# Offset weight tiles, two conversions moved beside the last block, and the second output step's sums moved into the h stage

## The chip, the cores and the metric

The kernel runs on one core of one Trainium2 chip. The metric is the device time of one execution in microseconds (us), lower is better. Five engines work side by side, each through its own list of instructions in order: PE (matmuls, with PEld for the weight loads), DVE and POOL (elementwise), ACT (elementwise, activations, casts) and SP, which here only issues transfers (DMAs). An instruction waits until what it reads has been written and what it overwrites has been read.

## The reference

The reference chains three pieces: an attention over a window of 64 keys (4 batches, 8 heads, 576 positions, head size 64), a bilinear layer and a SiLU layer, all on 2304 tokens of width 512.

```
scores = q @ k^T / 8, masked to 0 <= i - j < 64
x  = softmax(scores) @ v                    # 2304 x 512
x2 = ((x @ w1) * (x @ w2)) @ w3 @ w_out     # 512 -> 1024 -> 1024 -> 512
h  = x2 @ w_in                              # 512 -> 2048
y  = (h * sigmoid(h)) @ w_out2              # 2048 -> 512
```

`q`, `k`, `v` are single precision. The weights arrive in double precision and are turned into single precision on the chip.

## The kernel before

**Precision.** A single-precision product is made of rounded halves: each operand is split into a high part and a low remainder, and a product takes three passes (high by high, low by high, high by low). A weight tile therefore holds both halves of a 128x512 piece, and a matmul has 128 rows, 128 columns of weights and 384 tokens (256 output columns in the last stage).

**Conversion of a double-precision weight.** A tile of 64-bit words comes from DRAM (`l0`, `l1` issue the load, L145). ACT takes two ACTIVATEs over it (L220 writes `cv_b`, L225 writes `cv_r`), DVE masks and merges the bits (L228, then SCALAR_TENSOR_TENSOR at L884), POOL adds the remainder (L887). For `w_out2` the function `convert(n, at, places)` does this for a pair of tiles, adds the sums that the seven-product scheme wants (`cv_t`, `cv_u`) and stores all seven pieces to the DRAM scratch `t32`. Its pieces are entered in the table `jobs` at times from `at - 2` (first load) to `at + 7` (last store).

**Stages.** (1) to about 95 us: `w3` and `w_out` are folded into one weight `wp`, attention begins. (2) Six blocks of 384 tokens (`phase_a`): sixteen chains `ab` (x by w1 and w2, L693), whose even members are copied out by ACT (L707) and whose odd ones DVE multiplies with that copy; `p` is the split product; then four chains `x2` (L723) with `wp`, stored to DRAM. The chains rotate through four PSUM banks, so a chain waits until the copy or product of the fourth chain before it has read its bank. Attention of the next block is woven in; the last block (5) has none, and there `hooks5` brings in the first operands of the next stage: at unit 0 it loads `x2` of the earlier blocks (`xra`, `xe`) and the first `w_in` tile (`r`). A block has 24 units: one per `ab` chain, then two per `x2` chain. (3) The h stage, 462 to 639 us: 12 "duos" of 7 slots, each slot one product of 12 matmuls (L1016) of a seven-product scheme (the products in PSUM tiles `ha` to `hd`, read out by ACT and DVE to `gxa`, `gxb`, `gst` and stored to DRAM as `gd`). After each slot `run_jobs` issues what the table `jobs` holds for the slot's number: weight parts (`w_part`, `o_part`), operand splits (`x_op`, `x_sum`) and the pieces of the eight conversions. (4) The output stage: 36 steps `out_products` (L1160), each from one load of `gd` (`f_load`), its sums (`f_sums`, DVE) and its split halves (`f_high` on ACT, `f_low` on DVE).

**Order.** The engines' lists follow the order in which the Python code issues instructions. In block 5 the key of a job is `n5 + unit` with `n5 = -24`; in the h stage it is the slot number, 0 to 83. `PLAN` gives the conversions their times, `FIRST_OUT` (56) is the slot at which preparations for the output stage begin.

**Places.** Tiles of one tag share one place in SBUF over the kernel's life. The weight tiles have tags `w0` to `w23`, each 4096 bytes per partition, and come to lie in the order of their first use; all begin at multiples of 128 bytes. The pool `end`, opened before block 5, holds operand tiles `x0` to `x6`.

Of the kernel before, what the change touches and what calls it, by code (L numbers as in the profile page):

```python
# [9 lines left out]
F32 = mybir.dt.float32  # L10
# [32 lines left out]
def tile_window_attention_ffn(ctx, tc, qkv, qkp, vp, w1, w2, w3t, w_out, w_in, w_out2, out):  # L43
# [7 lines left out]
    nc = tc.nc  # L51
    main = ctx.enter_context(tc.tile_pool(name="main", bufs=1))
# [50 lines left out]
    def slot(name, tag, dims, dtype=F32, pool=None, bufs=1):  # L103

        t = (pool or main).tile([128, SLOTS.get(tag, 1024)], dtype, name=name, tag=tag, bufs=bufs)
        n = int(np.prod(dims))
        letters = "abcd"[: len(dims)]
        sizes = {x: d for x, d in zip(letters[1:], dims[1:])}
        return t[:, :n].rearrange(f"p ({' '.join(letters)}) -> p {' '.join(letters)}", **sizes)
# [628 lines left out]
    def new_pt():  # L738
        for i in range(4):
            n = 128 if i // 2 else 64  # L740
            pt[i % 2, i // 2] = att.tile([128, 512], F32R, name=f"pt{i}", tag=f"pt{i}", bufs=1)[:, : 4 * n].rearrange(
                "p (h t n) -> p h t n", h=2, t=2
            )
        for i in range(2):
            for h, hs in HEADS:
                nc.gpsimd.memset(f32(pt[i, 0][hs, 1 - h]), 0.0)

    with tc.manual_schedule():
        xr = slot("xr", "xr", [4, NB])
        xe = slot("xe", "xe", [2304])  # L750
        phase_w()
        new_pt()
        chunks = []
        for i in range(16):
            qq, k = divmod(i, 4)
# [28 lines left out]
        end = ctx.enter_context(tc.tile_pool(name="end", bufs=1, side="right"))  # L784
        PAIRS = FF2 // 256
# [16 lines left out]
        def add(eng, out, a, b):  # L802
            tt(eng, out, a, b, ALU.add)

        def sub(eng, out, a, b):
            tt(eng, out, a, b, ALU.subtract)

        def run_later():
            for f in later[:]:
                later.remove(f)  # L810
                f()
# [109 lines left out]
        def at(n, f, *args):  # L921
            jobs.setdefault(n, []).append(lambda: f(*args))
# [167 lines left out]
        def f_sums(m, eng=None):  # L1090

            if m < NTG * DUOS:
                f, t = [x.rearrange("p (a n) -> p a n", a=4) for x in raw["f", m]]
                add(eng or nc.gpsimd, t[:, 0], f[:, 3], f[:, 2])
                sub(nc.vector, t[:, 1], f[:, 3], f[:, 0])
                sub(nc.vector, t[:, 2], t[:, 0], f[:, 0])
                sub(nc.vector, t[:, 3], f[:, 1], t[:, 2])

        def f_high(m):
            if m < NTG * DUOS:
                n = m % 4
                if n == 3:
                    lo = slot(f"lo{m}", "xa", [6, 256], F32R)
                    a = unit_tile("wo", 6, 3)[:, 0:512]
                else:
                    if "a11" not in tmp:
                        tmp["a11"] = slot("a11", "xr", [3, 512], F32R)
                    lo = slot(f"lo{m}", ("x2", "x4", "x0")[n], [6, 256], F32R, end)  # L1110
                    a = tmp["a11"][:, n]
                hi = slot(f"hi{m}", ("x1", "x3", "x5", "x6")[n], [6, 256], F32R, end)
                a = [a[:, 0:256], a[:, 256:512]]
                sets[m] = lo, hi, a
                f, t = raw["f", m]
                for i, x in ((0, f), (3, t)):
                    nc.scalar.copy(out=hi[:, i : i + 3], in_=x[:, 0:768].rearrange("p (a n) -> p a n", a=3))
                nc.scalar.copy(out=a[0], in_=t[:, 768:1024])
# [119 lines left out]
        n5 = -24  # L1238
# [9 lines left out]
        for j in range(1, SUPER):  # L1248
# [5 lines left out]
                at(s + k, *((f, j, x) if f is x_op else (f, x)))  # L1254
            for k, x in ((13, 4), (14, 5), (17, 6)):
                at(s + k, x_op, j, x)
        PLAN = tuple((n, 12 + 5 * n) for n in range(PAIRS))
        FIRST_OUT = 7 * DUOS * (SUPER - 1)
        for n, first in ((0, 2), (1, 10), (2, 12), (3, 16), (4, 18), (5, 23), (6, 26)):
            for part in range(4 if n < 6 else 2):  # L1260
                at(FIRST_OUT + first + part, o_part, n, part)
        for n, first in ((0, 0), (1, 6), (2, 6), (3, 13), (4, 16), (5, 20), (6, 22)):
            at(FIRST_OUT + first, o_load, n)
        for k, f, m in ((22, f_load, 0), (22, f_load, 1), (25, f_high, 0), (26, f_low, 0)):
            jobs.setdefault(FIRST_OUT + k, []).insert(0, lambda f=f, m=m: f(m))
        jobs.setdefault(FIRST_OUT + 24, []).insert(0, lambda: f_sums(0, nc.vector))
        at(FIRST_OUT + 26, f_load, 2)
        at(FIRST_OUT + 27, o_load, 7)

        phase_a(NBLK - 1, hooks5)  # L1270
        mid.close()
        pso = ctx.enter_context(tc.tile_pool(name="pso", bufs=1, space=PSUM, reuse_waits="tile"))
# [3 lines left out]
        def thirds(t):  # L1276
            return t.rearrange("p (t q n) -> p t q n", t=3, q=2)

        tmp["q"] = slot("gq", "q", [2304])
        xb, xa = slot("gxb", "xb", [2, 768]), slot("gxa", "xa", [2, 768])  # L1280
# [1 line left out]
        homes = [xb[:, 0], xb[:, 1], xa[:, 0], xa[:, 1], st[0][:, 0:768], st[1][:, 0:768]]  # L1282
        names = ("one", "a22", ("two", 1), "a11", "a12", ("two", 0))
        g.update((n, thirds(t)) for n, t in zip(names, homes))
        for i, (n, first) in enumerate(PLAN):
            convert(n, first, [tmp["q"][:, 0:1024], tmp["q"][:, 1024:2048]])
        for d in range(NDUO):
            for pos in range(7):
                h_slot(d, pos)
        run_later()  # L1290
        f_sums(1, nc.vector)
        f_high(1)
        f_low(1)
        out_products(0)
# [105 lines left out]
```

## Time and profile before

| | |
|---|---|
| median of 3 runs | 829.37 us (829.13 to 831.34) |
| profiled execution, own time | 831.39 us |
| its span, first to last instruction | 829.6 us |
| granted TensorE clock, mean | 0.998 |
| PE busy | 811.6 us, 98% of the span |
| DVE, ACT, POOL busy | 79%, 66%, 47% |
| block 5 | 411.8 to 461.7 us |
| h stage | 461.9 to 639 us |

The span is counted from the first instruction to the last; the execution's own time has 1.8 us more around it. Matmul ends are modelled, so PE's busy share says that a matmul was in flight, not that every cycle of the array was used. A bracket behind a row gives the engine's idle time ahead of it and what released it.

### The profile page before, as it was taken

What the parts mean: (1) busy time and instruction counts of PE and PEld (TensorE: products, weight loads), DVE (VectorE), ACT (ScalarE), POOL (GpSimd) and SP (SyncE); (2) the same over time, 40 slices, a digit from 0 to 9 for tenths busy, and PEclk for the clock granted to TensorE, in tenths of its full rate; (3) what the DMA queues carried; (4) which work ended last, traced back from release to release, by engine and by line L of the source; (5) the groups of instructions that cost most, each with busy time, mean ns of one, the idle gap of its engine ahead of it and who ended that gap; (6) DMA issues with size and microseconds to landing.
All of it is one profiled execution on the core that took longest, in us unless ns stands there. A gap on an engine that the chain in (4) does not pass through costs nothing.

```text
span 829.6 us, 15630 instructions
## 1 busy us (share of the span) xinstructions
PE 811.6 (98%) x5066; PEld 766.6 (92%) x5066; DVE 653.8 (79%) x1527; ACT 543.7 (66%) x1290; POOL 389.8 (47%) x468
## 2 busy tenths in 40 slices
PE   8899999999999999999999999999999899999998
PEld 3455799999999999999999999999999899999998
DVE  7878867788888888888557579977657999888882
ACT  6889878888899898899645456654555543444330
POOL 4768576667677677677644126444000112221100
PEclk9999999999999999999999999999999999999999
DMA  9998324534444545544132377896867555444421
GB/s 287 338 316 267 106 75 122 169 114 154 157 146 155 169 134 160 176 143 137 72 111 96 133 267 243 294 323 268 303 226 246 178 152 154 146 134 129 127 77 51
DMA packets 79792, 146.34 MB, mean 176 GB/s; under 512 B 7136, under 2 KB 46432, under 8 KB 79712
## 3 DMA queue, kind: packets, MB, share of 16 engines
q1 hardware_dynamic: 76112, 140.50, 51.7%
q10 hardware_dynamic: 3600, 4.85, 1.6%
q8 instruction: 40, 0.66, 0.3%
q14 instruction: 40, 0.33, 0.1%
HBM read 105.48 MB, written 39.85 MB: 175 GB/s over the span
## 4 chain that ended last, share of the span: by engine, by line
PE 66%; DVE 7%; ACT 7%; POOL 6%; issue 5%; DMA 1%; ACTq 0%; SPq 0%; DVEq 0%; POOLq 0%
PE ab L693 15%; PE oa L1160 11%; PE x L723 8%; PE ob L1160 8%; PE ha L1016 4%; PE hb L1016 4%; PE hd L1016 4%; PE hc L1016 2%; PE accw L614 2%; POOL klo L351 2%; PE t L428 2%; POOL vhl L369 1%; POOL p L117 1%; PE o L462 1%; POOL xr L474 1%
## 5 line engine op out<-in xcount | busy, mean ns | idle before, releaser
L693 PE MATMUL ab<-xa,hl 128*128 128x384 f32 x576 | 119.0, 341 | 0.0
L693 PE MATMUL ab<-xb,hl 128*128 128x384 f32 x570 | 115.2, 334 | 0.0
L693 PEld LDWEIGHTS ab<-xb,hl 128*128 128x128 f32 x570 | 100.3, 188 | 0.0
L693 PEld LDWEIGHTS ab<-xa,hl 128*128 128x128 f32 x576 | 99.1, 188 | 0.0
L1160 PE MATMUL oa<-wo_w,hi 128*128 128x256 f32 x408 | 77.9, 285 | 0.0
L351 POOL TENSOR_TENSOR klo<-qk,qkhi 64x192 fp32r<-64x192 f32 x110 | 67.3, 612 | 8.4 <-ACT qkhi L345 2.3
L723 PE MATMUL x<-p,wp 128*128 128x384 f32 x360 | 69.0, 339 | 0.0
L474 POOL TENSOR_TENSOR xr<-ot 128x128 f32<-128x128 f32 x55 | 32.7, 595 | 72.9 <-DVE ot L473 54.5
L800 POOL TENSOR_TENSOR fs<-f 128x256 f32<-128x256 f32 x11 | 9.8, 889 | 121.2 <-DMA f<-gd 99.7
L1160 PEld LDWEIGHTS oa<-wo_w,hi 128*128 128x128 f32 x408 | 63.6, 191 | 0.0
L723 PEld LDWEIGHTS x<-p,wp 128*128 128x128 f32 x360 | 61.8, 188 | 0.0
L1160 PE MATMUL oa<-wo_w,lo 128*128 128x256 f32 x204 | 58.3, 286 | 0.4 <-DVE lo L800 0.4
L406 ACT ACTIVATE sm<-sm,nm 128x192 f32<-128x192 f32 x110 | 49.3, 449 | 1.4
L1016 PE MATMUL ha<-xop,wi_w 128*128 128x384 f32 x252 | 47.8, 335 | 0.7 <-ACT gxb L1038 0.7
L1016 PE MATMUL hd<-xop,wi_w 128*128 128x384 f32 x252 | 47.7, 335 | 0.5 <-DVE gxb L800 0.5
L1016 PE MATMUL hb<-xop,wi_w 128*128 128x384 f32 x252 | 47.5, 334 | 0.0
L345 ACT CAST qkhi<-qk 128x768 fp32r<-128x768 f32 x55 | 46.0, 835 | 1.2
L392 DVE CUSTOM_DVE_ANT_0 sm<-s,consts 128x192 f32<-128x192 f32 x144 | 45.2, 352 | 1.3 <-PE s L385 0.8
L1016 PEld LDWEIGHTS ha<-xop,wi_w 128*128 128x128 f32 x252 | 44.0, 188 | 1.2 <-ACT gxb L1038 1.2
L1016 PEld LDWEIGHTS hd<-xop,wi_w 128*128 128x128 f32 x252 | 43.9, 188 | 0.8 <-DVE gxb L800 0.8
L1016 PEld LDWEIGHTS hb<-xop,wi_w 128*128 128x128 f32 x252 | 44.0, 188 | 0.0
L428 PE MATMUL t<-consts,sm 128*128 128x128 f32 x216 | 35.9, 275 | 7.4 <-DVE sm L418 5.3
(284 smaller groups left out, 2331.7 us busy)
## 6 DMA issues: line engine op xcount, KB each, us to landing
qk<-in_qkv SPq DMA_DIRECT2D x55, 384.0 KB, 3.0
words<-in_w3t SPq DMA_DIRECT2D x16, 512.0 KB, 6.4
words<-in_w SPq DMA_DIRECT2D x16, 512.0 KB, 6.6
xe<-in_w_in SPq DMA_DIRECT2D x16, 512.0 KB, 4.6
gq<-in_w_out SPq DMA_DIRECT2D x16, 512.0 KB, 4.5
gd<-gxa SPq DMA_DIRECT2D x18, 384.0 KB, 3.3
gd<-gst SPq DMA_DIRECT2D x18, 384.0 KB, 5.1
gq<-gd SPq DMA_DIRECT2D x13, 512.0 KB, 4.0
```

What stands on the lines that cost most here:

```text
L345: nc.scalar.copy(out=hi, in_=t)
L351: nc.gpsimd.tensor_tensor(out=k_lo[g % 2][hs, h * 192 : h * 192 + 192], in0=t[hs, n], in1=f32(hi[hs, n]), op=ALU.subtract)
L392: nc.vector.tensor_tensor_reduce(out=sm[g % 2][:, h, :], in0=s_ps[:, h, :], in1=consts[:, at + 64 - 64 * h : at + 256 - 64 * h], op0=ALU.a ...
L406: nc.scalar.activation(out=e[:, h, :], in_=x, func=AF.Exp, scale=-1.0, bias=nm[:, h : h + 1], accum_out=sums_of[g % 2][:, h, 0:1])
L428: nc.tensor.transpose(t_ps[:, i * 128 : i * 128 + 128], x[:, at : at + 128], id_sb)
L474: nc.gpsimd.tensor_tensor(out=xr[:, c, r : r + 128], in0=t[:, 0:128], in1=t[:, 128:256], op=ALU.add)
L614: nc.tensor.matmul(acc[i], lhsT=w3x[s % 7][:, i * 128 : (i + 1) * 128], rhs=wo[:, j], start=(j == 0), stop=(j == 7))
L693: nc.tensor.matmul(acc, lhsT=w[:, l, fs], rhs=x[k // 2][:, k % 2, r, :], start=(k == 0 and n == 0), stop=(k == 3 and n == 2),)
L723: nc.tensor.matmul(acc, lhsT=wp[f][:, l, o * 128 : (o + 1) * 128], rhs=p[f][:, r, :], start=(f == 0 and n == 0), stop=(f == 7 and n == 2),)
L800: eng.tensor_tensor(out=out, in0=a, in1=b, op=op)
L1016: nc.tensor.matmul(bank[name][:, q, 0:NB], lhsT=w[:, l, first + kt], rhs=x[:, kt, r, :], start=(fresh and kt == 0 and n == 0), stop=(kt == ...
L1160: nc.tensor.matmul(dst, lhsT=lhs[l], rhs=rhs[r], start=(first and e == 0 and q == 0 and n == 0), stop=(e == DUOS - 1 and q == 1 and n == 2 ...
```

## The change

Three edits. **First**, ahead of all other tiles the tags `p`, `q`, `xa` and `xb` get their places, then 24 times a filler tile of 32 bytes followed by a weight tag, so that the weight tiles begin 32, 64, 96 and 0 bytes behind a multiple of 128 in turn. Only addresses change. **Second**, conversions 0 and 1 of `w_out2` move from slots 12 and 17 of the h stage to units 2 and 7 of block 5, with the words in `x4` and `x5` of the pool `end`; the other six start at slots 13 + 5n, one slot later than before. **Third**, the load of output step 1 goes from slot 78 to slot 70 (at 78 it stood ahead of the load of step 0, since both were put in at the front of the list), and its sums go from behind the last h slot to slot 72, on DVE.

```diff
--- before.py
+++ after.py
@@ -748,6 +748,11 @@
     with tc.manual_schedule():
         xr = slot("xr", "xr", [4, NB])
         xe = slot("xe", "xe", [2304])
+        for t in ("p", "q", "xa", "xb"):
+            slot(f"first_{t}", t, [1])
+        for i in range(24):
+            main.tile([128, 8], F32, name=f"gap{i}", tag=f"gap{i}")
+            slot(f"first_w{i}", f"w{i}", [1])
         phase_w()
         new_pt()
         chunks = []
@@ -1254,19 +1259,23 @@
                 at(s + k, *((f, j, x) if f is x_op else (f, x)))
             for k, x in ((13, 4), (14, 5), (17, 6)):
                 at(s + k, x_op, j, x)
-        PLAN = tuple((n, 12 + 5 * n) for n in range(PAIRS))
+        PLAN = tuple((n, 13 + 5 * n) for n in range(2, PAIRS))
         FIRST_OUT = 7 * DUOS * (SUPER - 1)
         for n, first in ((0, 2), (1, 10), (2, 12), (3, 16), (4, 18), (5, 23), (6, 26)):
             for part in range(4 if n < 6 else 2):
                 at(FIRST_OUT + first + part, o_part, n, part)
         for n, first in ((0, 0), (1, 6), (2, 6), (3, 13), (4, 16), (5, 20), (6, 22)):
             at(FIRST_OUT + first, o_load, n)
-        for k, f, m in ((22, f_load, 0), (22, f_load, 1), (25, f_high, 0), (26, f_low, 0)):
+        at(FIRST_OUT + 14, f_load, 1)
+        at(FIRST_OUT + 16, f_sums, 1, nc.vector)
+        for k, f, m in ((22, f_load, 0), (25, f_high, 0), (26, f_low, 0)):
             jobs.setdefault(FIRST_OUT + k, []).insert(0, lambda f=f, m=m: f(m))
         jobs.setdefault(FIRST_OUT + 24, []).insert(0, lambda: f_sums(0, nc.vector))
         at(FIRST_OUT + 26, f_load, 2)
         at(FIRST_OUT + 27, o_load, 7)
 
+        for i in range(2):
+            convert(i, n5 + 2 + 5 * i, [slot(f"cw{i}_{x}", x, [1024], pool=end) for x in ("x4", "x5")])
         phase_a(NBLK - 1, hooks5)
         mid.close()
         pso = ctx.enter_context(tc.tile_pool(name="pso", bufs=1, space=PSUM, reuse_waits="tile"))
@@ -1282,13 +1291,12 @@
         homes = [xb[:, 0], xb[:, 1], xa[:, 0], xa[:, 1], st[0][:, 0:768], st[1][:, 0:768]]
         names = ("one", "a22", ("two", 1), "a11", "a12", ("two", 0))
         g.update((n, thirds(t)) for n, t in zip(names, homes))
-        for i, (n, first) in enumerate(PLAN):
+        for n, first in PLAN:
             convert(n, first, [tmp["q"][:, 0:1024], tmp["q"][:, 1024:2048]])
         for d in range(NDUO):
             for pos in range(7):
                 h_slot(d, pos)
         run_later()
-        f_sums(1, nc.vector)
         f_high(1)
         f_low(1)
         out_products(0)
```

PE's list is the same in both kernels, row for row. On the other engines the rows differ from block 5 on. In the pieces below a row is line, operation, result and operands, shape; the lines of the changed kernel are five higher from L751 on.

ACT, the first chains of block 5: `ab_0`, `ab_2`, `ab_4` are even chains, `a` their copies, `p` their split products, `xop` an operand of the h stage, `cw_x` a converted tile's words. Before:

```order
L701 COPY a_0_5667<-ab_0_5655 128x384
L114 CAST p_5648<-a_0_5667 128x384
L707 COPY a_1_5700<-ab_2_5687 128x384
L971 CAST xop_0_5702<-xra_5650 128x2x384
L114 CAST p_5648<-a_1_5700 128x384
L707 COPY a_2_5735<-ab_4_5722 128x384
```

and now:

```order
L701 COPY a_0_5724<-ab_0_5712 128x384
L114 CAST p_5704<-a_0_5724 128x384
L220 ACTIVATE cv_b<-cw_x_5700 128x512
L225 ACTIVATE cv_r<-cw_x_5700 128x512
L707 COPY a_1_5762<-ab_2_5749 128x384
L976 CAST xop_0_5764<-xra_5706 128x2x384
L220 ACTIVATE cv_b<-cw_x_5701 128x512
L114 CAST p_5704<-a_1_5762 128x384
L225 ACTIVATE cv_r<-cw_x_5701 128x512
L707 COPY a_2_5804<-ab_4_5791 128x384
```

Two ACTIVATEs of conversion 0 stand ahead of the copy of `ab_2`, and two of its second tile ahead of the copy of `ab_4`. They read the tile that a load brings.

SP, the transfers of block 5 (`xra`, `xe` are `x2`, `r` is a `w_in` tile, `t` is the scratch `t32`). Before:

```order
L979 DMA xra_5650<-x2d 128x2x768
L979 DMA xe<-x2d 128x2x768
L843 DMA r_5653<-w_in_76 128x4x256
L843 DMA r_5906<-w_in_76 128x4x256
L843 DMA r_5949<-w_in_76 128x4x256
```

and now:

```order
L984 DMA xra_5706<-x2d 128x2x768
L984 DMA xe<-x2d 128x2x768
L848 DMA r_5709<-w_in_76 128x4x256
L145 DMA cw_x_5700<-in_w_out 128x1024
L145 DMA cw_x_5701<-in_w_out 128x1024
L145 DMA cw_x_5702<-in_w_out 128x1024
L145 DMA cw_x_5703<-in_w_out 128x1024
L913 DMA t_5699<-cv_b 128x512 x2
L916 DMA t_5699<-cv_t 128x512
L917 DMA t_5699<-cv_u 128x256
L913 DMA t_5699<-cv_b 128x512 x2
L848 DMA r_6012<-w_in_76 128x4x256
```

The loads of the words stand behind those of `xra`, `xe` and the first `r`; the second `r` now comes behind nearly all stores of conversions 0 and 1.

DVE in the h stage, from slot 17 on: `wi_p` and `wi_w` are weight tiles, `hb` and `hd` products in PSUM. Before:

```order
L800 TENSOR_TENSOR gst_6121<-hb_1_6399,gxb 128x768
L800 TENSOR_TENSOR wi_w_6291<-gst_6122,wi_w_6291 128x512
L800 TENSOR_TENSOR gst_6123<-gst_6123 128x2x128
L228 TENSOR_SCALAR cv_b<-cv_b 128x512
L800 TENSOR_TENSOR gxa<-hd_5_6351,gxa 128x768
L800 TENSOR_TENSOR gst_6123<-gst_6123 128x2x128
L884 SCALAR_TENSOR_TENSOR cv_b<-gq,cv_b 128x512
L800 TENSOR_TENSOR cv_t<-cv_b 128x256
L800 TENSOR_TENSOR wi_p<-gst_6123,wi_p 128x512
L800 TENSOR_TENSOR cv_t<-cv_b,cv_t 128x256
L228 TENSOR_SCALAR cv_b<-cv_b 128x512
L800 TENSOR_TENSOR gxb<-hb_1_6399,gxb 128x768
```

and now:

```order
L805 TENSOR_TENSOR gst_6229<-hb_1_6494,gxb 128x768
L805 TENSOR_TENSOR wi_w_6399<-gst_6230,wi_w_6399 128x512
L805 TENSOR_TENSOR gst_6231<-gst_6231 128x2x128
L805 TENSOR_TENSOR gxa<-hd_5_6453,gxa 128x768
L805 TENSOR_TENSOR gst_6231<-gst_6231 128x2x128
L805 TENSOR_TENSOR wi_p<-gst_6231,wi_p 128x512
L805 TENSOR_TENSOR gxb<-hb_1_6494,gxb 128x768
```

Five instructions of conversions 0 and 1 are gone from between the weight parts and the read-outs of `hb` and `hd`.

DVE near the h stage's end, where output step 1 is summed (`xe`) and split (`lo`). Before:

```order
L800 TENSOR_TENSOR gxb<-hd_5_7761,gxb 128x768
L800 TENSOR_TENSOR wo_w_7755<-or_7669,wo_w_7755 128x512
L800 TENSOR_TENSOR xe<-xe 128x256 x4
L800 TENSOR_TENSOR lo_7785<-xe,hi_7786 128x768 x2
L800 TENSOR_TENSOR a_7725<-xe,a_7725 128x256
L800 TENSOR_TENSOR wo_w_7756<-or_7669,wo_w_7756 128x512
```

and now, eight slots earlier for the sums:

```order
L805 TENSOR_TENSOR wo_w_7494<-gq,wo_w_7494 128x256
L805 TENSOR_TENSOR gxa<-hd_5_7536,gxa 128x768
L805 TENSOR_TENSOR xe<-xe 128x256 x4
L805 TENSOR_TENSOR wo_w_7607<-gst_6230,wo_w_7607 128x512
L805 TENSOR_TENSOR wo_w_7608<-gst_6230,wo_w_7608 128x512
L805 TENSOR_TENSOR gxb<-hb_1_7577,gxb 128x768
```

The four instructions of the sums stand among the read-outs and weight parts of slot 72; behind the last slot the split follows the weight part `wo_w` directly.

## Rows read from the trace of the kernel before

**Rows 1.** Page, busy time (share of the span) and instructions of each engine.

```profile
PE 811.6 (98%) x5066; PEld 766.6 (92%) x5066; DVE 653.8 (79%) x1527; ACT 543.7 (66%) x1290; POOL 389.8 (47%) x468
```

**Rows 2.** Windows: start:end, length, then busy PE, PEld, DVE, ACT, POOL, clock, DMA share, GB/s.

```profile
403.00:461.90 58.90, 58.90 (x344) 58.90 (x342) 34.46 (x51) 28.51 (x57) 29.73 (x28) 1.00 0.31 101
...
663.00:820.00 157.00, 157.00 (x1311) 157.00 (x1310) 130.63 (x226) 59.53 (x100) 28.03 (x29) 1.00 0.41 125
```

**Rows 3.** Chain of waits, longest steps: start, length, engine, result, line, count.

```profile
415.61 29.64 PE ab L693 x171
...
665.48 2.88 PE oa L1160 x24
```

**Rows 4.** Waits of PE from 95 us on: who for whom, sum, count, largest.

```profile
PE ob L1160 <- DVE lo L800: 2.5, 2, 1.7
```

**Rows 5.** SP's queue at 414 us (start, length, issue), and landing of L843 there.

```profile
415.30 0.36 SPq L843 DMA_DIRECT2D r<-w_in  x1
...
DMA to landing us min/median/max: 8.8/8.8/8.8
```

**Rows 6.** Landing of the word loads (L145) between 470 and 540 us.

```profile
DMA to landing us min/median/max: 3.3/4.5/6.1
```

**Rows 7.** Windows, columns as in rows 2: transfers while words are loaded.

```profile
490.00:495.00 5.00, 5.00 (x30) 5.00 (x29) 3.24 (x7) 5.00 (x10) 0.45 (x2) 1.00 1.03 417
```

**Rows 8.** Timeline of ACT: start, busy, line, operation; a conversion's pair, and block 5.

```profile
489.72 0.66 ACT L220 ACTIVATE cv_b<-gq 128x512 f32<-128x512 f32 x1
490.28 0.67 ACT L225 ACTIVATE cv_r<-gq 128x512 int32<-128x512 uint32 x1
...
418.24 0.48 ACT L707 COPY a<-ab 128x384 f32<-128x384 f32 x1 [0.92 <-PE ab L693]
```

**Rows 9.** Timeline of PE in block 5, the chain that reuses the bank of `ab_2`.

```profile
424.28 1.20 PE L693 MATMUL ab<-xa,hl 128*128 128x384 f32 x6
```

**Rows 10.** Timeline of PE at the stall of the output stage.

```profile
657.51 0.39 PE L1160 MATMUL ob<-wo_w,lo 128*128 128x256 f32 x1 [1.67 <-DVE lo L800]
```

**Rows 11.** Windows: behind that stall, and at a wait early in the kernel.

```profile
659.50:662.90 3.40, 3.40 (x18) 3.40 (x17) 3.33 (x7) 2.46 (x4) 1.60 (x2) 0.50 0.39 136
...
20.00:28.00 8.00, 6.13 (x21) 2.95 (x20) 6.28 (x19) 6.42 (x17) 4.69 (x5) 1.00 1.05 337
```

**Rows 12.** Timeline of PE in the h stage at its three waits.

```profile
506.45 0.51 PE L1016 MATMUL hb<-xop,wi_p 128*128 128x384 f32 x2
507.37 0.97 PE L1016 MATMUL hb<-xop,wi_p 128*128 128x384 f32 x4 [0.41 <-DVE wi_p L800]
508.84 2.37 PE L1016 MATMUL hd<-xop,wi_w 128*128 128x384 f32 x12 [0.50 <-DVE gxb L800]
...
524.57 1.21 PE L1016 MATMUL hd<-xop,wi_p 128*128 128x384 f32 x6
526.49 2.37 PE L1016 MATMUL ha<-xop,wi_w 128*128 128x384 f32 x12 [0.72 <-ACT gxb L1038]
```

**Rows 13.** Timelines of DVE, ACT and PE: a conversion's step, and a read-out just in time.

```profile
567.14 0.69 DVE L884 SCALAR_TENSOR_TENSOR cv_b<-gq,cv_b 128x512 int32<-128x512 int32 x1
...
584.06 0.79 ACT L1038 COPY gxb<-ha 128x768 f32<-128x768 f32 x1
...
584.90 1.33 PE L1016 MATMUL ha<-xop,wi_w 128*128 128x384 f32 x6
```

**Rows 14.** Timelines of DVE, PE and ACT at the end of the h stage.

```profile
632.72 1.55 DVE L800 TENSOR_TENSOR gq<-gq 128x256 f32<-128x256 f32 x4 [2.84 <-DMA gq<-gd]
...
634.96 1.20 PE L1016 MATMUL hd<-xop,wi_w 128*128 128x384 f32 x6
...
635.39 0.95 DVE L800 TENSOR_TENSOR gxb<-hb,gxb 128x768 f32<-128x768 f32 x1
...
641.72 1.55 DVE L800 TENSOR_TENSOR xe<-xe 128x256 f32<-128x256 f32 x4
...
642.50 1.56 ACT L1117 CAST hi<-xe 128x768 fp32r<-128x768 f32 x2
```

## Prediction

> **What bounds the kernel now.** I read the page's busy times first: PE is busy for 98% of the span, the next engine, DVE, for 79% [rows 1]. Block 5 and the output stage were read as windows: in both PE is busy in every microsecond at full clock, while the others are at half load or less, DVE in the output stage excepted [rows 2]. The chain of waits says how fast a busy PE goes: 171 matmuls of 384 columns in 29.64 us are 173.3 ns each, 24 of 256 columns in 2.88 us are 120.0 ns [rows 3]. The 53.3 ns between the two are 128 columns at one per cycle of 2.4 GHz, so 384 columns take 160 ns and 13.3 ns per matmul are something else. PE's list does not change. So the time moves for two reasons only: PE waits more or less, or a matmul's 173.3 ns become another number. From 95 us on PE waits little; its longest waits are at the start of the output stage, 2.5 us in two [rows 4].
>
> **Block 5, conversions 0 and 1.** ACT takes its list in order, so the two ACTIVATEs ahead of the copy of `ab_2` make it wait for the words, and the copy is what frees the bank for `ab_6`. Before, that copy ran at 418.24 [rows 8] and PE came to the bank at 424.28 [rows 9]: 424.28 less the end 418.72 is 5.6 us of slack. When do the words land? Their load stands behind `r`, issued at 415.30, which took 8.8 us to land [rows 5]: 424.1. Its 512 KB at the 417 GB/s of a busy stretch [rows 7] are 1.26 us: 425.4. The two ACTIVATEs start 0.56 apart [rows 8], so the copy begins 1.1 later, at 426.5, and ends at 427.0. PE, due at 424.28, waits **2.8 us**. Bounds: if the two transfers go side by side and the words land with `r` at 424.1, the wait is 1.5; if they need 3.3 us behind it, the quickest landing of a word load elsewhere [rows 6], it is 4.8. The wait is nothing if they land by 422.6. I take the 2.8 because the queue is one and `r` is the nearest row. Block 5 has no other wait that this could be hidden in [rows 2].
>
> Behind a wait the clock may fall. After the stall of 1.67 us at 657.51 [rows 10] it stood at 0.50 for 3.4 us [rows 11], that is 1.2 GHz. At half clock 384 columns take 173.3 ns more, so a stretch of 3.4 us does the work of 1.7 us and costs **1.7 us**. Against it: early in the kernel PE was idle for 1.87 of 8 us and the clock stayed at 1.00 [rows 11]. I take the fall, since the wait is longer than the one that brought it.
>
> The Trainium skill, "TensorE: Matmul & The Clock Gate", Part 1 (The HAM clock gate), says that the throttled clock is the default and that recent activity of PE releases it. By that rule a new idle stretch in a stage that has none speaks against this edit: it costs more than its length. The stretch behind 657.51 agrees (0.50), the early one does not (1.00) [rows 11].
>
> The rest of these conversions lies beside work: ACT and DVE stand at 28.5 and 34.5 of 58.9 us [rows 2], and their pieces of four tiles (two ACTIVATEs of 0.6 and two or three DVE steps of 0.4 to 0.7 each) are about 8 us over thirteen units. If the cover fails, it does so at the second `r`: its load is now behind conversion 1's stores on SP, and the weight casts from it stand in ACT's list ahead of the last split that an `x2` chain needs. I take 0; at worst 1.5 us.
>
> **The h stage without them.** PE waits three times there in the slots where conversions 0 and 1 stood: 0.41, 0.50 and 0.72 us, for a `wi_p` remainder and two read-outs of PSUM [rows 12]. From start to start less 173.3 ns per matmul: 507.37 less 506.45 less two is 0.57; 508.84 less 507.37 less four is 0.78; 526.49 less 524.57 less six is 0.88. All three are read-outs or remainders behind conversion steps on DVE or ACT; with those gone I expect all to go: **-2.2 us** (between 0 and -2.4, with restarts). Next late is what runs one slot later now: at 584.06 ACT copies `ha` for 0.79 us and ends at 584.85, and PE goes on at 584.90 [rows 13]: no slack. One conversion step of 0.69 us [rows 13] may come to stand ahead of that read-out; I take half, **+0.35** (0 to 0.7).
>
> The Trainium skill, "SBUF — State Buffer", section Who interferes with whom, says that a DVE instruction with two SBUF inputs contends with a POOL instruction that reads SBUF. Fewer such pairs in the h stage would by that rule be a further small gain in DVE's time; it reaches PE only where PE waits, and those waits are counted above.
>
> **The end of the h stage.** `f_load(0)` no longer stands behind `f_load(1)`. DVE idled 2.84 us for it before the sums at 632.72 [rows 14], so these end earlier; but the read-out of `hb` behind them, at 635.39, then waits for PE's last `hb` matmul, which the next chain follows at 634.96: the gain is 0.43 at most, and I take **-0.25**. The sums of step 1, 1.55 us at 641.72, lay beside ACT, which began the cast `hi` at 642.50 [rows 14]; `lo` on DVE needs `hi`, so taking the sums away frees DVE earlier than ACT lets it go on. 0, at best -0.3. The stall at 657.51 hangs on later `lo`s and stays.
>
> **The offsets.** No row of before shows a weight tile off a multiple of 128, so this is bounded from both sides. 1152 `ab`, 576 `x2` and 864 h matmuls have such weights; three of four are moved. If the 13.3 ns came from where the tile lies and went: 2592 x 3/4 x 13.3 ns = 26 us less. As much more is not excluded by a row. I take 0: the 13.3 ns are the same at 384 and at 256 columns, for weights from other tiles and for weights from activations (in the output stage the weights are `hi` and `lo`, and the moving side is `wo_w`), which looks like a fixed step between two matmuls.
>
> The same skill section says that PE has two read ports of its own and waits for no other engine; by that rule addresses against other engines' traffic change nothing and the sum stays.
>
> **Sum.** 831.39 (the profiled execution, span 829.6 and 1.8 around it) + 2.8 + 1.7 - 2.2 + 0.35 - 0.25 = 833.8. That execution was 2.02 above the median of 829.37, so the forecast is **831.8 us**, 2.4 above before. This is just inside 0.3% (2.5 us), about what a measurement of this kernel can tell from no change.
>
> **Rivals and chances.**
>
> - The forecast, 0.45. Its own range goes from 829.9 (the wait at 1.5, a shorter fall) to 834.2 (the wait at 4.8): half of it same, half slower.
> - PE waits in block 5 but the clock holds, as it did at 26 us: 831.8 - 1.7 = 830.1. 0.20, nearly all same.
> - The words land by 422.6, as word loads elsewhere do in 3.3 to 6.1 us [rows 6], if the 8.8 of `r` is a late start of its own and not a full queue: no wait, no fall. 829.37 - 2.2 + 0.35 - 0.25 = 827.3. 0.17, half of it faster. Against it: one queue, 8.8 us ahead.
> - The offsets shorten the 13.3 ns; the edit then decides, from 1.3 ns per moved matmul on (1944 x 1.3 ns = 2.5 us). A third of the 13.3 would give 831.8 - 8.6 = 823. 0.09. For it: 13.3 ns have no cause that the trace names. Against it: they are equal wherever I measured them.
> - They lengthen it by as much: 840. 0.04, slower.
> - On the other side, a further wait in block 5: the second `r` lands late behind the stores, ACT's casts from it hold up the split `p` of the seventh pair, and the `x2` chain waits up to 1.5 us. It decides from 0.1 us on, as the forecast is so near the bound; 831.8 + 1.5 = 833.3. 0.05, slower.
>
> Faster by over 0.3%: 0.08 + 0.09 + 0.01 = 0.18. Slower: 0.23 + 0.01 + 0.04 + 0.05 = 0.33. Within: 0.49. The range is 826.2 to 834.2: it leaves out most of the offset cases and the upper tail of the forecast, together less than 2 in 10.
>
> **What would show it.** In the changed trace: a wait of PE at `ab_6` in block 5, ended by ACT's copy, of 1.5 to 4.8 us, and ahead of it on ACT an ACTIVATE on `cw_x` released by its load; a window behind it with the clock at 0.50; no wait of PE on `wi_p` or the read-outs near slots 21 to 30; DVE's sums in `gq` at the h stage's end no longer released by a DMA so late; the stall of `ob` on `lo` unchanged. Wrong would be: 171 `ab` matmuls in a time other than 29.64 us (offsets matter), a word load that lands in under 7 us (no wait), or a clock of 1.00 behind the wait.

## The result: slower by 1.2%

The changed kernel takes 840.05 us (median of 5 runs, 839.6 to 841.31) against 830.06 us before on the same chip (829.13 to 831.34, 5 runs): a ratio of 1.0124, 95% interval 1.0109 to 1.0138. The forecast was 831.8 us in a range of 826.2 to 834.2. The profiled execution took 841.31 us with a span of 839.3, 9.7 us longer than the span before.

The page's busy times of the changed kernel, against [rows 1]:

```profile
PE 815.4 (97%) x5066; PEld 770.0 (92%) x5066; DVE 652.5 (78%) x1527; ACT 542.7 (65%) x1290; POOL 391.5 (47%) x468
```

No engine has more to do, and the shares are those of before within one point. Starts of the same matmuls in both traces tell where the time went:

| stretch | changed less before, us |
|---|---|
| up to the first chain of block 5 | -0.59 |
| block 5 (first chain to first matmul of the h stage) | +12.56 |
| h stage | +0.12 |
| output stage, to the last matmul | -2.45 |

The first row is already there at the first of the six blocks (-1.04), and kernels that are that of before up to block 5 have it too (f4_plan15 -1.38, h3_order -0.46): it is no effect of the change. The loss is block 5. Waits of PE in it, in the changed kernel (sum, count, longest; before, the same stretch had none [rows 2]):

```profile
PE x L723 <- ACT q L114: 3.2, 2, 3.1
PE ab L693 <- DVE a L709: 2.1, 2, 1.7
PE ab L693 <- ACT a L707: 1.6, 1, 1.6
PE x L723 <- POOL q L117: 0.9, 1, 0.9
```

Where they stand, in PE's timeline (the chain at 425.64 is the one of [rows 9]):

```profile
425.64 1.32 PE L693 MATMUL ab<-xa,hl 128*128 128x384 f32 x6 [1.60 <-ACT a L707]
...
441.13 1.31 PE L693 MATMUL ab<-xa,hl 128*128 128x384 f32 x6 [0.33 <-DVE a L709]
...
447.32 1.32 PE L693 MATMUL ab<-xa,hl 128*128 128x384 f32 x6 [1.74 <-DVE a L709]
...
454.48 0.44 PE L723 MATMUL x<-q,wp 128*128 128x384 f32 x1 [0.85 <-POOL q L117]
458.02 1.01 PE L723 MATMUL x<-q,wp 128*128 128x384 f32 x2 [3.10 <-ACT q L114]
```

Behind the last one the clock fell, as a window shows (columns as in [rows 2]); behind the first it did not:

```profile
426.00:431.00 5.00, 5.00 (x30) 5.00 (x29) 4.77 (x5) 2.26 (x5) 3.64 (x2) 1.00 0.36 105
...
458.50:463.50 5.00, 5.00 (x17) 5.00 (x17) 3.90 (x7) 2.53 (x6) 2.52 (x3) 0.51 0.42 149
```

17 matmuls start in the 5 us, where 30 did in the window above. At half clock (1.2 GHz) six matmuls of 384 columns take 1.92 us from start to start, 320 ns each:

```profile
458.82 2.12 PE L723 MATMUL x<-p,wp 128*128 128x384 f32 x6
460.74 0.53 PE L729 MATMUL x<-q,wp 128*128 128x384 f32 x1
```

That is 384 columns at 1.2 GHz with nothing on top: the 13.3 ns of the full clock are not there. By the starts, the 12.56 us are: 1.95 up to `ab_6`, 0.28 to `ab_9`, 0.65 to `ab_13`, 2.03 to `ab_15`, 0.13 to the first `x2` chain, 5.30 in it, 2.12 in the second one (the clock), 0.10 in the rest.

What each wait hangs on. ACT's timeline, the row of [rows 8] among them:

```profile
424.00 0.66 ACT L220 ACTIVATE cv_b<-cw_x 128x512 f32<-128x512 f32 x1 [7.21 <-DMA cw_x<-in_w_out]
424.56 0.66 ACT L225 ACTIVATE cv_r<-cw_x 128x512 int32<-128x512 uint32 x1
425.12 0.47 ACT L707 COPY a<-ab 128x384 f32<-128x384 f32 x1
...
456.63 0.62 ACT L861 CAST wi_w<-r 128x512 fp32r<-128x512 f32 x1 [2.56 <-DMA r<-w_in]
457.15 0.40 ACT L862 CAST wi_w<-r 128x256 fp32r<-128x256 f32 x1
457.46 0.51 ACT L114 CAST q<-a 128x384 fp32r<-128x384 f32 x1
```

The words landed behind `r`, as their places in SP's queue have it. The loads with their issue times, then the time to landing of `r` and of the first words:

```profile
414.69 0.36 SPq L848 DMA_DIRECT2D r<-w_in  x1
415.11 18.63 SPq L145 DMA_DIRECT2D cw_x<-in_w_out  x4
...
DMA to landing us min/median/max: 8.0/8.0/8.0
...
DMA to landing us min/median/max: 8.9/8.9/8.9
```

The copy that frees the bank stands behind ACT's wait for the words, and the last split `q` behind a wait for the second `w_in` tile. That tile is late on SP's queue, where the store of conversion 1 waits ahead of it for POOL:

```profile
451.69 0.81 SPq L913 DMA_DIRECT2D t<-cv_b  x2
452.59 0.40 SPq L848 DMA_DIRECT2D r<-w_in  x1
```

DVE and POOL are late themselves. Two rows of DVE first, then three of POOL:

```profile
429.58 2.07 DVE L228 TENSOR_SCALAR cv_b<-cv_b 128x512 int32<-128x512 int32 x1
...
440.99 1.79 DVE L805 TENSOR_TENSOR xop<-xe,xop 128x768 fp32r<-128x768 f32 x1
```

```profile
428.80 2.56 POOL L805 TENSOR_TENSOR xra<-xe,xra 128x768 f32<-128x768 f32 x1
...
440.68 1.29 POOL L892 TENSOR_TENSOR cv_b<-cv_b,cv_r 128x512 int32<-128x512 int32 x1 [1.57 <-DVE cv_b L889]
...
447.35 2.00 POOL L892 TENSOR_TENSOR cv_b<-cv_b,cv_r 128x512 int32<-128x512 int32 x1
```

The TENSOR_SCALAR takes 0.41 to 0.43 us where POOL is idle at its start (424.69 and 444.73 in this trace); here it ends at 431.65, just behind POOL's instruction (431.36). That one (`xra`) is not of the conversions. The `xop` at 440.99 began beside POOL's add for conversion 1 (440.68 to 441.97).

In the h stage the three waits of [rows 12] are gone, which is worth 2.25 us between the chain `hb` that began at 505.41 before and the `ha` of 526.49. A new wait takes 0.92 of it back, with its restart:

```profile
594.26 1.31 PE L1021 MATMUL hd<-xop,wi_w 128*128 128x384 f32 x6 [0.76 <-DVE gxb L805]
```

It waits for DVE's read-out of the `hd` before, with a step of a conversion (`cv_t`) ahead of it:

```profile
592.91 0.42 DVE L805 TENSOR_TENSOR cv_t<-cv_b,cv_t 128x256 f32<-128x256 f32 x1
593.25 0.95 DVE L805 TENSOR_TENSOR gxb<-hd,gxb 128x768 f32<-128x768 f32 x1
```

The rest of the gain goes into the slower pace of 384 columns (e1_offsets below): 1008 matmuls at 1.4 ns are 1.4 us.

The stall of [rows 10] is there as before (1.83 us, 1.67 before). The output stage is faster without any wait less: it does more matmuls in the same time. The same window in the kernel before and in the changed one:

```profile
700.00:800.00 100.00, 100.00 (x836) 100.00 (x835) 87.00 (x152) 38.25 (x65) 20.23 (x21) 1.00 0.44 136
```

```profile
700.00:800.00 100.00, 100.00 (x847) 100.00 (x846) 87.40 (x156) 39.27 (x65) 20.75 (x22) 1.00 0.46 141
```

100 us by 836 are 119.6 ns, by 847 they are 118.1 ns.

### The profile page after: what moved, and what is told of

Its sections match the earlier page's. It is cut to its first block, busy times and chain, and to the rows that moved or that the text cites. A ratio compares the mean times of both kernels' runs of the same rounds, so it can differ in the third digit from the quotient of the medians.

```text
span 839.3 us, 15624 instructions
## 1 busy us (share of the span) xinstructions
PE 815.4 (97%) x5066; PEld 770.0 (92%) x5066; DVE 652.5 (78%) x1527; ACT 542.7 (65%) x1290; POOL 391.5 (47%) x468
## 4 chain that ended last, share of the span: by engine, by line
PE 64%; ACT 8%; DVE 7%; POOL 5%; issue 5%; DMA 4%; ACTq 0%; SPq 0%; DVEq 0%; POOLq 0%
PE ab L693 13%; PE oa L1165 11%; PE x L723 8%; PE ob L1165 8%; PE ha L1021 5%; PE hb L1021 4%; PE hd L1021 4%; PE hc L1021 2%; PE t L428 2%; DMA gq<-in_w_out 2%; PE accw L614 2%; POOL klo L351 1%; DMA cw_x<-in_w_out 1%; PE o L462 1%; PE s L381 1%
## 5 line engine op out<-in xcount | busy, mean ns | idle before, releaser
L723 PE MATMUL x<-p,wp 128*128 128x384 f32 x360 | 71.8, 349 | 0.0
L723 PEld LDWEIGHTS x<-p,wp 128*128 128x128 f32 x360 | 64.4, 194 | 0.0
L723 PE MATMUL x<-q,wp 128*128 128x384 f32 x210 | 41.6, 339 | 4.1 <-ACT q L114 3.2
```

The lines of the kernel that those rows point to most:

```text
L723: nc.tensor.matmul(acc, lhsT=wp[f][:, l, o * 128 : (o + 1) * 128], rhs=p[f][:, r, :], start=(f == 0 and n == 0), stop=(f == 7 and n == 2),)
```

## The experiments

Ratios are against the kernel before in the same series, with their 95% intervals.

**The three parts apart.** e1_offsets has only the first edit, e2_conv only the second, e3_sums only the third, and e4_no_gaps is the whole change with this line taken out:

```diff
         for i in range(24):
-            main.tile([128, 8], F32, name=f"gap{i}", tag=f"gap{i}")
             slot(f"first_w{i}", f"w{i}", [1])
```

> Only the offsets, nothing else of the change. Theory A (the loss is waits in block 5 that the two conversions bring): within 1.5 us of before; PE never waits in block 5; the 384-column matmuls go from 173.5 to about 174.9 ns (some 2700 of them, +3.8 us) and the 256-column ones from 120.0 to about 118.4 ns (1512, -2.4 us). Theory B (the offsets slow the elementwise engines and the matmuls, and block 5 only shows it): slower by 4 us or more, with waits in block 5 without any conversion there.

Measured: 830.4 us, 0.9993 (0.9985 to 1.0002). No wait in block 5. Its chain there, against the 29.64 us of [rows 3], in the chain of waits:

```profile
414.47 29.91 PE ab L693 x171
```

That is 174.9 ns per matmul. Theory A holds.

> Only the two conversions in block 5, all weight tiles at multiples of 128. Theory A: slower than before by 9 to 12 us: block 5 about 12 us longer with PE's waits at ab_6, ab_13, ab_15 and in the first x2 chain as in the changed kernel, the three waits of the h stage gone (-2.4), new ones of about 1.2 near 593 us. Theory B: slower by less than 5 us.

Measured: 841.28 us, 1.0131 (1.0116 to 1.0147), block 5 longer by 13.4 us. PE waits 2.7 us at `ab_6`, 1.2 at `ab_15`, 3.6 and 0.9 in the first `x2` chain, and not at `ab_13`. The second edit alone brings the whole loss. Here the clock fell at `ab_6` too (window, columns as in [rows 2]):

```profile
426.21:429.62 3.41, 3.35 (x10) 3.35 (x11) 3.14 (x4) 2.68 (x6) 1.61 (x2) 0.50 0.00 0
```

> Only the earlier load and sums of output step 1. Both theories: 0 to 0.6 us faster, from the first wait of the output stage (0.98 before, about 0.7 then); the wait at ob on lo of 1.8 us stays. A rival: DVE's sums in slot 72 delay a read-out and cost as much, no change.

Measured: 830.48 us, 0.9997 (0.9988 to 1.0006). In the trace the waits of PE's `ob` for `lo` are 2.2 us together instead of 2.5, as the first of them, near the start of the output stage, is 0.59 instead of 0.82; the last matmul comes 0.3 us sooner, counted from the first block, less than the times can tell.

> The whole change without the 24 filler tiles: the tags get their places in the same order, but every weight tile begins at a multiple of 128 again. If the matmul times come from the offsets, 384 columns are at 173.5 and 256 columns at 120.0 ns again, and the time is about 1 us from the changed kernel's. If they come from where the tiles lie (the new order), they stay at 174.9 and 118.4. The waits of block 5 stay in both.

Measured: 840.32 us, 1.0115 (1.0101 to 1.0128); 384 columns at 173.6, 256 columns at 119.96 ns. The matmul times come from the offsets, not from the order of the tiles, and the loss from neither.

**What in the conversions costs.** f1_late_stores issues the stores of conversion 1 seven units later, f2_words_first loads the words of conversion 0 ahead of all else, f3_both does both:

```diff
-            for k, f in (... (6, store_b), (7, store_t)):
+            s = 7 if n == 1 else 0
+            for k, f in (... (6 + s, store_b), (7 + s, store_t)):
...
+        run_jobs(n5)
+        run_jobs(n5 + 1)
         phase_a(NBLK - 1, hooks5)
```

> The changed kernel with the four stores of conversion 1 issued seven units later, behind the loads of the second and third w_in tile on SP. Theory A1 (SP's queue holds the second w_in tile, ACT's cast of it holds the split that the first x2 chain needs, and the clock falls behind that wait): the 3.4 us wait in the first x2 chain and the half clock behind it go, 4 to 6 us less than the changed kernel; the waits at ab_6, ab_13 and ab_15 stay. Theory A2 (DVE and POOL are too slow with both conversions, whatever SP does): less than 1.5 us less.

Measured: 839.21 us, 1.0097 (1.0075 to 1.012), by the ratios 2.2 us less than the changed kernel, between the two theories. The last wait shrinks from 3.1 to 2.0 us only, and the clock falls as before: `q` now waits for DVE's product `a` (ACT idles 1.46 us for it) and not for the tile. The wait at `ab_6` was 2.3 us here, so block 5 as a whole is 0.26 us shorter than in the changed kernel, and its first `x2` chain 1.1: A1 is a small part.

> The changed kernel with the words of conversion 0 loaded ahead of the other transfers of block 5. If ACT's wait for the words starts the trouble (the copy of ab_2 late, all of DVE's list behind it late by 7 us): the wait at ab_6 goes (-1.9) and those at ab_13 and ab_15 shrink to nothing (-2.7), so 4 us or more less than the changed kernel. If only the head of the line is meant: 1.9 less, the rest as before. The wait in the first x2 chain stays in both.

Measured: 837.04 us, 1.0075 (1.0056 to 1.0093). The wait at `ab_6` is gone and that at `ab_13` too; `ab_15` still waits 1.6, the `x2` chain 3.2 and 0.9 us. Block 5 is 2.8 us shorter, and the wait of the h stage at 594 is gone although the lists there are the same. By the ratios the kernel is 4 us faster than the changed one, as the first theory has it, but `ab_15` keeps most of its wait: the late start does not carry on into all that follows.

> Both edits of the two runs before: words of conversion 0 first, stores of conversion 1 late. If the two causes are all of the loss of block 5, PE waits there for at most 1 us and the kernel is at 827 to 829, faster than before by the three waits of the h stage that are gone. If DVE and POOL are too slow with the conversions, ab_13, ab_15 and the x2 chain still wait and it is at 832 or more.

Measured: 834.92 us, 1.0053 (1.0036 to 1.007). Waits of PE in block 5:

```profile
PE x L723 <- ACT q L114: 2.1, 2, 2.0
PE ab L693 <- DVE a L709: 1.6, 1, 1.6
PE x L723 <- POOL q L117: 0.9, 1, 0.9
```

Both queues mended, block 5 still loses 7.74 us (this execution took 836.44, above the median). A third cause is left, the largest.

> As the run with words first and late stores, but only conversion 0 in block 5; conversion 1 is back in the h stage (slot 18). Theory C (what is left of the loss, 7.7 us in block 5, is that DVE and POOL hold each other up with both conversions' instructions between the weight parts from unit 8 on): the waits at ab_15 and in the first x2 chain (1.8, 1.0, 2.3 us) and the half clock go, block 5 loses under 2 us: 829 to 831. Rival D (it is ACT's list, two more pairs of ACTIVATEs per conversion ahead of copies and casts): half of it stays, 832 to 834.

Measured: 828.83 us, 0.9985 (0.9973 to 0.9998). No wait of PE in block 5, which loses 0.77 us (the run with the offsets alone lost 0.48 there). With one conversion there is room.

> As the run with words first and late stores, with both conversions in block 5, but their DVE and POOL instructions left out (loads, ACTIVATEs and stores stay; the two pairs of w_out2 are not converted). Theory C: block 5 loses under 1 us against before, 826 to 829. Rival D (ACT) or E (the transfers): the wait in the first x2 chain of 2.3 us stays with its half clock, 831 to 833.

Measured: 828.25 us, 0.9976 (0.9967 to 0.9986), no wait in block 5. ACT's and the transfers' part, D and E, costs nothing once the words come first and the stores late.

> As the run before this one, but only POOL's instructions of the two conversions are left out, DVE's stay. If DVE is slow because POOL works beside it (elementwise instructions of 0.95 us took 1.6 to 1.8 there): DVE's instructions go back to about 1 us and block 5 loses under 2 us, 827 to 830. If DVE's own number of instructions is too large: half of the 7.7 us or more stays, 831 to 834.

The edit, in each of three places:

```diff
-                nc.gpsimd.tensor_tensor(out=c.b, in0=c.b, in1=c.r, op=ALU.add)
+                if n > 1:
+                    nc.gpsimd.tensor_tensor(out=c.b, in0=c.b, in1=c.r, op=ALU.add)
```

Measured: 828.31 us, 0.9976 (0.9965 to 0.9987), no wait in block 5, which loses 0.7 us. DVE's instructions by line between 425 and 452 us (count, busy, mean ns), first with POOL's part (f3_both), then without (g3_no_pool):

```profile
L805 DVE TENSOR_TENSOR wi_w<-r,wi_w 128x512 fp32r<-128x512 f32 x3 | 4.5, 1497 | 0.0
...
L805 DVE TENSOR_TENSOR xop<-xe,xop 128x768 fp32r<-128x768 f32 x2 | 3.0, 1519 | 0.0
L228 DVE TENSOR_SCALAR cv_b<-cv_b 128x512 int32<-128x512 int32 x3 | 2.9, 965 | 0.0
```

```profile
L805 DVE TENSOR_TENSOR xop<-xe,xop 128x768 fp32r<-128x768 f32 x4 | 4.2, 1042 | 0.6 <-ACT xop L983 0.6
L805 DVE TENSOR_TENSOR wi_w<-r,wi_w 128x512 fp32r<-128x512 f32 x4 | 4.0, 991 | 0.4 <-ACT wi_w L861 0.4
...
L228 DVE TENSOR_SCALAR cv_b<-cv_b 128x512 int32<-128x512 int32 x3 | 1.3, 419 | 0.0
```

DVE has the same list in both. Without POOL's instructions many of its own are a third to over a half shorter, while others, as most SCALAR_TENSOR_TENSORs at L889 (0.68 us), are as long in both. The groups go by time and so hold different numbers; row for row, the 25 DVE instructions from `xra` to the product `a` of `ab_13` took 24.4 us in f3_both (from 425.83) and 19.3 in g3_no_pool (from 425.59). DVE was idle for 2.1 of the one and 1.7 of the other: it is late because its instructions are longer, not because it waits for POOL's results. The `xop` of the changed kernel at 440.99 (1.79 us) is this row of g3_no_pool, where POOL is idle from 433.29 to 436.79:

```profile
435.77 0.96 DVE L805 TENSOR_TENSOR xop<-xe,xop 128x768 fp32r<-128x768 f32 x1 [0.17 <-ACT xop L983]
```

POOL's own adds took 1.8 us each in f3_both, against 1.3 in the h stage of the kernel before:

```profile
L892 POOL TENSOR_TENSOR cv_b<-cv_b,cv_r 128x512 int32<-128x512 int32 x4 | 7.3, 1834 | 1.0 <-DVE cv_b L889 1.0
```

> The changed kernel, words and stores where it has them, with POOL's instructions of the two conversions left out (so the two pairs of w_out2 are wrong in value). If POOL is the root of nearly all: the wait at ab_6 for the words stays (1.9 us), those at ab_13, ab_15 and in the first x2 chain go, since the stores no longer wait and the second w_in tile is loaded in time: block 5 loses 2 to 3 us, 829.5 to 832. If the queue order on SP and the late start each cost by themselves: block 5 loses 5 us or more, 833 or above.

Measured: 831.95 us, 1.0017 (1.0007 to 1.0027). Waits in block 5:

```profile
PE ab L693 <- ACT a L707: 2.7, 1, 2.7
PE x L723 <- ACT q L114: 1.3, 1, 1.3
```

Block 5 loses 5.2 us instead of 12.6: POOL's instructions, out of the changed kernel with nothing else done, give back 7.3. The time lies in the range of the first theory, the loss of block 5 in that of the second, so the words and the late start cost something by themselves: 3.0 us up to `ab_6`, where the wait for the words is 2.7 here, and 1.6 in the first `x2` chain. There `q` waits for DVE's `a` (ACT idles 1.17 us for it) and not for the second tile. The clock stays at 1.00 behind both. So the 12.56 us of the changed kernel are 4.8 that go with the two queues (f3_both), 7.05 that go with POOL's instructions (g3_no_pool) and 0.69 that stay, most of it the offsets' pace (0.48 in e1_offsets).

**The offsets.** h2_uniform64 has one filler of 64 bytes ahead of `w0` in place of the 24 (the tiles behind the weights are moved by it too).

> The kernel before with the offsets of the change replaced by one filler of 64 bytes ahead of the first weight tile: all 24 begin 64 bytes behind a multiple of 128. If an offset as such makes the difference, 384 columns take about 174.9 and 256 columns about 118.4 ns as with the four offsets in turn; if it is the change from one offset to another, 173.5 and 120.0 as before. The time is within 1.5 us of before in both.

Measured: 831.07 us, 1.0001 (0.9991 to 1.0011). The window of the output stage and the chain of block 5 (window, chain of waits):

```profile
700.00:800.00 100.00, 100.00 (x847) 100.00 (x846) 87.53 (x154) 39.57 (x67) 20.00 (x21) 1.00 0.45 137
```

```profile
415.73 29.64 PE ab L693 x171
```

One offset for all speeds up the 256-column matmuls as four in turn do. For 384 columns the mean over the kernel is 174.9 ns, as with four offsets, though the chains of block 5 keep their 173.3 here; the slower ones are in the earlier blocks and in the h stage. Why it differs between them stays open.

**Towards a better kernel.** f4_plan15 is the kernel before with the third edit and the conversions' times moved by three slots, all in the h stage:

```diff
-        PLAN = tuple((n, 12 + 5 * n) for n in range(PAIRS))
+        PLAN = tuple((n, 15 + 5 * n) for n in range(PAIRS))
```

> The kernel before with the third part of the change, and all eight conversions kept in the h stage but begun three slots later, at 15 + 5n. If the three waits of the h stage (2.2 us) come from conversions 1 and 2 falling together with the last weight parts of w_in, they go without anything in block 5: 826.5 to 828.5. If they come from the conversions' own number of instructions, they move on to other slots: 829 to 831.

Measured: 828.34 us, 0.9971 (0.996 to 0.9982), the lowest ratio of the runs that leave no work out, though its interval overlaps those of g1_one_conv, g5_plan15_pool and i1_one_conv_plan15. The three waits of [rows 12] go, one of 0.7 us comes at 563.42, where before had none. In its profile the clock stays at 1.00 behind the stall, 1.7 us here, where it fell before [rows 11]:

```profile
656.00:661.00 5.00, 4.57 (x37) 4.38 (x36) 4.93 (x10) 2.97 (x6) 1.95 (x2) 1.00 0.33 105
```

> The run with all conversions in the h stage at 15 + 5n, and the three remainders of the last w_out2 pair (right behind the h stage) on POOL instead of DVE, where they stand ahead of the lo that PE waits for (1.8 + 0.6 us). About 2.3 us of DVE's work gone there: the stall shrinks by 1.5 to 2.4 us and with it the half clock behind it, where it comes: 825 to 827.5. If POOL's slower pace makes wo_p late instead, PE waits for wo_p and nothing is won: 828 to 829.

Measured: 828.5 us, 0.9977 (0.9968 to 0.9986). The remainders took POOL 5.91 us and the `lo` beside them 3.29 instead of 2.36; the stall only changes its place.

> All conversions in the h stage at 15 + 5n and the earlier sums of step 1 (828.3 in its run), and behind the h stage the sums and the split of output step 3 ahead of the last pair of w_out2 instead of behind it. DVE is idle there for 1.4 us until ACT has cast that pair, and the lo that PE waits for comes after it. Expected: the stall of 1.8 + 0.6 us shrinks by 1 to 2 us, 826 to 827.5; rival: PE waits for wo_p instead, 828 to 829.

Measured: 830.54 us, 1.0003 (0.9994 to 1.0012). The rival: PE waits for `wo_p` instead, twice 1.3 us, and the time is above the rival's range as well; its profile accounts for 0.7 us more of waits behind the h stage than f4_plan15 has, and the rest stays open.

> As the run before, with the offsets of the change. By the matmul times: 3.5 us more up to the end of the h stage, 2.4 less behind it, so 0.5 to 1.5 us slower than without; by the run with the offsets alone, which was level with before (0.9993), no difference.

Measured: 830.19 us, 0.9998 (0.9988 to 1.0008): no difference, as the run with the offsets alone.

> The kernel before with the earlier sums of step 1, conversion 0 alone in block 5 with its words loaded first, the other seven in the h stage at 15 + 5n, all tiles at multiples of 128. If block 5 has room for one conversion: no wait of PE there beyond 0.3 us, the waits of 0.9 and 0.3 us near 563 that the run with all eight in the h stage had are smaller or gone, 827 to 828.5. If one conversion costs there as much as it frees in the h stage: 828.5 to 830.

Measured: 828.87 us, 0.9982 (0.9973 to 0.9991). One wait in block 5 (0.5 us, ACT's `q`), 0.8 us lost there; the h stage waits less than in f4_plan15. It gives back what it saves.

## Why the prediction was wrong, step by step

- **The step that failed**: "The rest of these conversions lies beside work ... I take 0; at worst 1.5 us." It was argued from shares of busy time (ACT 28.5 and DVE 34.5 of 58.9 us) and from short durations of single instructions, as most had in the h stage of the kernel before (12 of 16 TENSOR_SCALARs took 0.41 to 0.43 us there, the others up to 0.96). POOL's 29.7 us, which stand in the same row [rows 2], were left out; "half load or less" is 59% for DVE and 50% for POOL there. POOL's part of two conversions, 8.7 us (a quarter of what the eight took in the h stage before), was left out too, and so was that DVE and POOL lengthen each other. Shown by g3_no_pool against f3_both (7.7 us lost in block 5, and 0.7 without POOL's part) and by h1_no_pool_alone (12.6 and 5.2). The Trainium skill, "SBUF — State Buffer", section Who interferes with whom, says that these two engines share a pair of ports, and that a DVE instruction with two SBUF inputs contends with POOL's reads. The trace agrees: the `xop` TENSOR_TENSOR, with both inputs in SBUF, took 0.96 us with POOL idle and 1.79 beside POOL's add; the TENSOR_SCALAR, which has one input, grew as well, from 0.42 to 2.07. The prediction read that rule for the h stage, as a gain, and not for block 5, where the same instructions went.
- **The wait at `ab_6`**: right in place and cause, step by step; 1.6 us idle (1.95 with restart) against 2.8. The words landed 1.29 us behind `r` (423.98 and 422.69; 1.26 was forecast), and the copy began 1.1 us later. But `r` took 8.0 us to land and not 8.8, and was issued 0.6 us earlier. In h1_no_pool_alone `r` took 9.1 us and the wait was 2.7. So the size hangs on the landing of `r`, which took 7.9 to 9.1 us in the five runs with this order of loads.
- **The half clock**: it came in another place, and the size was too small. The clock held behind the 1.6 us at 425.64 and fell within the 3.1 us before 458.02; PE then worked 5.4 us at half clock, not 3.4, which cost about 2.4 us, not 1.7. Behind a wait of 2.7 us at `ab_6` it fell in e2_conv and held in h1_no_pool_alone. At half clock a matmul of 384 columns takes 147 ns more (320 less 173.3), not 173.3.
- **The second `w_in` tile**: the mechanism of the last rival happened, behind the store as described, but the wait was 3.1 us and not 1.5, as the store waited for POOL. f1_late_stores shows that without it 2.0 us would have stayed, for DVE's late product.
- **The h stage**: -2.2 came as -2.25. The read-out that becomes late next cost 0.9 with its restart rather than 0.35. It is DVE's of `hd`, ahead of the chain at 582.78 before, and not ACT's of `ha` at 584.06. As f2_words_first has the same lists there and no such wait, the lists alone don't make it; what else does stays open.
- **The end of the h stage**: -0.25 came as -0.25: the first wait of the output stage is 0.57 us instead of 0.82 (0.59 in e3_sums).
- **The offsets**: 0 was right for the sum (0.9993) and wrong for the reason. The 13.3 ns are no fixed step: they became 14.9 at 384 columns and 11.7 at 256, and they are gone at half clock. The two changes of pace nearly cancel. The bounds counted 2592 matmuls and left out the 1512 of the output stage, whose moving side `wo_w` lies in the same tiles; the gain was there.
- **The rivals**: the words did not land in time, and PE did not keep its clock in the end. The rival on the slow side (0.05) happened together with the forecast's wait and a fall of the clock, at twice its price; that DVE and POOL are themselves too slow there was no rival at all. That the rival of slower offsets had 840 us, as measured, is luck: the offsets alone changed nothing. The upper end of the forecast's own range is 833.8 by its sum (2.0 us more of wait than 831.8 has), not 834.2.

## What to carry to other kernels

Free time of an engine is no room when another engine makes its instructions longer: before moving elementwise work there, look at DVE and POOL together, and in the trace for the same instruction with and without the other beside it. Their sum alone sets no bound here: between 411.5 and 461.5 us DVE and POOL were busy for 64.8 us together with one conversion (g1_one_conv), which cost next to nothing, and for 69.5 with two (f3_both), which cost 7.7. A moved step brings its whole list along (the wait of its first instruction on ACT, its stores on SP), and each stands ahead of something that was in time; move one step first and see whether the next still fits. Short waits that come from a coincidence of two tables can go by shifting one table by a few slots, as the three of [rows 12] did in f4_plan15.

## What the runs showed that was not expected

- Where the tiles begin changes the pace of PE with nothing waiting: all at multiples of 128 bytes, 173.6 and 119.96 ns per matmul of 384 and 256 columns (e4_no_gaps), with hardly any spread at 256 (a standard deviation of 0.4 ns); with offsets 174.9 and 118.4, with one of 2.5.
- The same wait left the clock at either level. Behind the stall of 1.7 us at the start of the output stage it stood at 0.50 in the kernel before and at 1.00 in f4_plan15, which is worth 1.5 us there, 1.1 of it still at the last matmul. Early in the kernel, PE's wait of 1.87 us left it at 1.00 in the kernel before [rows 11], and behind the same wait ahead of the same matmul, with the same lists up to there, it stood at 0.50 for 3.4 us in h3_order, g5_plan15_pool and i1_one_conv_plan15 (the window of [rows 11], in h3_order):

```profile
20.00:28.00 8.00, 6.13 (x19) 3.17 (x18) 6.16 (x18) 6.54 (x18) 4.80 (x4) 0.84 1.04 342
```

The prediction's case against a fall of the clock was one draw of this.
